# Splitting the second stage of a long convolution and its output stage into two halves of the channels

## The chip, the cores and the metric

The kernel runs on one core of one Trainium2 chip. The metric is the device time of one execution in microseconds (us). The kernel before takes 388.5 us (median of its first three runs, 388.43 to 392.61). Executions of the same kernel differ by 2 to 3 us either way, so smaller differences are read here from the traces and not from the times.

## The reference, cut to what matters

The output is two independent layers side by side, each 2048 steps by 1024 channels, in bf16.

```python
# A (H3): a long convolution over time, for each channel
kv  = shift(k, shift_k) * v                       # four taps
y_f = rfft(kv, 4096) * rfft(ssm_k, 4096)
a   = q * (irfft(y_f)[:2048] + kv * ssm_D)
# B (S5): a complex diagonal recurrence
Bu   = x @ B_bar.T
h[t] = Lam_bar * h[t-1] + Bu[t]
b    = 2 * (h @ C.T).real + x * Dskip
out  = concatenate([a, b], axis=-1)
```

## The kernel before

Layer A is a Fourier transform of length 4096 = 256 x 16, made of matmuls:

- Stage one transforms the signal (`am`) and the filter (`hm`) over the 256 and stores both in DRAM.
- Stage two takes 32 groups of frequencies. For each it loads both spectra, finishes the transform (`sh` filter, `sk` signal), swaps the real and imaginary partition halves of the filter spectrum by a transfer (`sw`), multiplies on VectorE (`pr`), transforms back (`sa`) and stores the inverse spectrum (`vst`).
- The output stage loads the inverse spectra (`vl`) and q (`ql`), does the last matmuls (`a3`), multiplies by q (`qm`, `qp`) and stores (`ost`, `oth`).

Layer B runs in 16 chunks of 128 steps: input projection `U`, rotation and scan on VectorE (`r1` to `r4`, `sc`), output projection `y`. It fills TensorE while layer A waits. ScalarE copies most results of TensorE out to SBUF (an "eviction"). A hand-written list of tasks fixes the order, and each engine runs its instructions in that order.

```python
ORDER = """ ... sk.31.0 sk.31.1 sae.28.1 y.12.0.0 cy.12 ske.31.0 ske.31.1 sa.29.0 sa.29.1 sae.29.0 sa.30.0 pr.31
sae.29.1 sa.30.1 sae.30.0 vst.14 sae.30.1 sa.31.0 sa.31.1 sae.31.0 y.12.0.1 sae.31.1 U.13.3 vst.15 U.15.0 ... """

def l_(nm, Ys, gq):                      # spectra of two groups, all 1024 channels: 512 KB
    if nm == "l2h":
        st[nm, gq] = btile("hk", [P, GC, D])
    else:
        st[nm, gq] = ap_pool("a2").tile([P, GC, D], BF16, name=nm, bufs=c["l2"])
    spd(st[nm, gq][:], Ys.rearrange("c n (s g) d -> (c n s) g d", g=NG)[:, gq * GC:(gq + 1) * GC, :])

def sw(g):                               # the swap, issued by GpSimd
    hab = st["hab", g]
    gpd(hab[0:64, 1, :], hab[64:128, 0, :])
    gpd(hab[64:128, 1, :], hab[0:64, 0, :])

def pr(g):                               # the product, on VectorE
    hab = st["hab", g]
    nc.vector.tensor_mul(hab[:], st.pop(("x16", g))[:].unsqueeze(1).to_broadcast([P, 2, D]), hab[:])

# ... cut ...
for task in ORDER.split():
    name, *a = task.split(".")
    E[name](*map(int, a))
```

`spd` issues a transfer from SyncE, `gpd` from GpSimd. The buffers of stage two (pool `a2`) and those of the output stage (pool `a3`) share the same memory, one after the other.

## Time and profile before

| | before |
|---|---|
| time, median | 388.5 us |
| span of the profiled execution | 386.9 us |
| TensorE / VectorE / ScalarE busy | 92% / 85% / 72% |
| work of TensorE, counted from the spacing of back-to-back matmuls | 352.2 us |
| span not filled by that work ("loss") | 34.7 us |

TensorE is the bound, so the question for any change is where TensorE stands still. The prediction shows the busy rows. Two further rows of the page: the clock granted to TensorE, in tenths for 40 slices, and the count of DMA packets.

```profile
PEclk9999999999999999999999999999999999999999
DMA packets 60506, 101.15 MB, mean 261 GB/s; under 512 B 28451, under 2 KB 31523, under 8 KB 60464
```

### The profile page before, as it was taken

Reading aid. Unit: us, or ns where it says so; the run is one execution under the profiler, and the core shown is the slowest. Engines: PE = TensorE matmul, PEld = TensorE weight load, DVE = VectorE, ACT = ScalarE, POOL = GpSimd, SP = SyncE. Lnnn points to the kernel's source line nnn. Section 1 sums busy time; section 2 is a strip of 40 time slices with the busy share of each in tenths; the row PEclk is TensorE's granted clock in tenths of the full one; section 3 lists DMA queues with packets and bytes.
Section 4 is the critical chain, followed back from the end, with each engine's and each line's share of the span. In section 5 each row is a group of like instructions: output and inputs, shape, how many; then the busy total and the mean of one; then the engine's idle time right before and its main releaser. Section 6 shows DMA issues by size and latency. Waiting matters only on the chain.

```text
span 386.9 us, 8963 instructions
## 1 busy us (share of the span) xinstructions
PE 357.3 (92%) x3509; PEld 244.7 (63%) x3553; DVE 329.4 (85%) x341; ACT 279.2 (72%) x511; POOL 128.1 (33%) x223
## 2 busy tenths in 40 slices
PE   2798998989999998999979999999997999999995
PEld 1587997859587765778536555465553676864442
DVE  2799999999999999999389999995943793989944
ACT  3799579786968698964867888868897876245331
POOL 7001004355555548661323324323442331011220
PEclk9999999999999999999999999999999999999999
DMA  7998299998775935456899999989997643998984
GB/s 243 372 347 295 86 221 298 269 327 271 285 215 196 284 154 207 186 178 222 260 300 290 307 271 319 272 296 268 322 271 259 226 154 133 324 401 267 393 302 163
DMA packets 60506, 101.15 MB, mean 261 GB/s; under 512 B 28451, under 2 KB 31523, under 8 KB 60464
## 3 DMA queue, kind: packets, MB, share of 16 engines
q1 hardware_dynamic: 46512, 58.21, 50.0%
q0 software_dynamic: 13872, 42.35, 30.3%
q8 instruction: 28, 0.46, 0.5%
q14 instruction: 14, 0.11, 0.1%
q10 hardware_dynamic: 80, 0.01, 0.0%
HBM read 53.10 MB, written 33.55 MB: 224 GB/s over the span
## 4 chain that ended last, share of the span: by engine, by line
PE 71%; ACT 9%; DMA 8%; DVE 6%; issue 4%; POOL 0%; DVEq 0%; ACTq 0%
PE ps_u L468 24%; PE ps_y L524 22%; PE ps_a L716 6%; PE ps_a L674 6%; DMA hab<-hab 3%; PE ps_a L746 3%; PE ps_a L593 2%; PE ps_a L639 2%; PE ps_y L529 2%; DMA CT<-in_B_B_im_dram 2%; PE ps_t L617 2%; ACT BT L434 2%; DMA Ys_h<-ysbh 1%; PE ps_t L422 1%; ACT ysbh L647 1%
## 5 line engine op out<-in xcount | busy, mean ns | idle before, releaser
L524 PE MATMUL ps_y<-CT,h 128*128 128x512 bf16 x478 | 130.1, 379 | 2.8 <-ACT yo L539 1.6
L468 PEld LDWEIGHTS <-BT 128*128 128x128 bf16 x2048 | 118.2, 98 | 8.7 <-ACT BT L434 1.3
L468 PE MATMUL ps_u<-xT,BT 128*128 128x128 bf16 x2048 | 122.7, 219 | 0.8 <-ACT BT L434 0.8
L524 PEld LDWEIGHTS <-h 128*128 128x128 bf16 x512 | 46.9, 98 | 46.7 <-issue 0.2
L500 DVE TENSOR_TENSOR_SCAN h<-rtab,h 128x1024 bf16<-128x1024 f32 x32 | 71.5, 2275 | 0.2
L470 ACT CAST u<-ps_u 128x512 bf16<-128x512 f32 x64 | 38.1, 595 | 41.3 <-PE ps_u L468 41.3
L707 DVE TENSOR_TENSOR hab<-x,hab 128x2048 bf16<-128x2048 bf16 x32 | 38.5, 1220 | 24.2 <-DMA hab<-hab 15.9
L654 POOL DMA_DIRECT2D Ys_h<-ysbh x64 | 45.4, 713 | 33.4 <-ACT ysbh L647 33.2
L480 DVE TENSOR_TENSOR mt<-u,Z 128x4096 bf16<-128x4096 bf16 x16 | 36.6, 2285 | 9.4 <-ACT u L470 9.4
L727 ACT CAST vsb<-ps_a 128x512 bf16<-128x512 f32 x64 | 36.8, 600 | 10.5 <-PE ps_a L716 7.6
L647 ACT CAST ysbh<-ps_a 128x512 bf16<-128x512 f32 x64 | 36.4, 619 | 8.2 <-DMA Ys_h<-ysbh 5.6
L604 POOL DMA_DIRECT2D Ys_kv<-ysb x32 | 17.8, 557 | 65.3 <-ACT ysb L602 64.9
L696 ACT CAST x<-ps_a 128x512 bf16<-128x512 f32 x64 | 36.8, 598 | 3.1 <-PE ps_a L674 2.9
L602 ACT CAST ysb<-ps_a 128x512 bf16<-128x512 f32 x64 | 36.4, 611 | 3.5 <-PE ps_a L593 3.5
L716 PE MATMUL ps_a<-hab,wts 128*128 128x512 bf16 x122 | 34.8, 379 | 4.2 <-DVE hab L707 4.1
L684 ACT CAST hab<-ps_a 128x512 bf16<-128x512 f32 x64 | 36.4, 600 | 2.1 <-PE ps_a L674 1.9
L701 POOL DMA_DIRECT2D hab<-hab x32 | 16.9, 527 | 60.1 <-ACT hab L684 59.7
L480 DVE TENSOR_TENSOR mt<-h,Z 128x4096 bf16<-128x4096 bf16 x16 | 36.6, 2286 | 0.2
L569 DVE TENSOR_TENSOR mt<-kring,wbc 128x4096 bf16<-128x4096 bf16 (+3 forms) x16 | 30.1, 1881 | 0.0
L539 ACT CAST yo<-ps_y 128x512 bf16<-128x512 f32 x32 | 19.1, 598 | 15.1 <-PE ps_y L524 15.1
L529 PE MATMUL ps_y<-Dd,xT 128*128 128x128 bf16 x128 | 28.0, 219 | 0.6
L639 PE MATMUL ps_a<-hT,F1t 128*128 128x256 bf16 x128 | 21.7, 272 | 1.6 <-ACT ysb L602 0.8
(118 smaller groups left out, 453.8 us busy)
## 6 DMA issues: line engine op xcount, KB each, us to landing
Ys_kv<-ysb POOLq DMA_DIRECT2D x32, 256.0 KB, 2.8
Ys_h<-ysbh POOLq DMA_DIRECT2D x64, 128.0 KB, 3.1
hk<-Ys_h SPq DMA_DIRECT2D x16, 512.0 KB, 6.3
l2k<-Ys_kv SPq DMA_DIRECT2D x16, 512.0 KB, 5.1
hab<-hab POOLq DMA_DIRECT2D x64, 128.0 KB, 4.2
Vs<-vsb POOLq DMA_DIRECT2D x16, 512.0 KB, 4.7
vv<-Vs SPq DMA_DIRECT2D x32, 256.0 KB, 5.5
hk<-in_A_ssm_k_dram SPq DMA_DIRECT2D x8, 512.0 KB, 4.8
```

The lines of the kernel that those rows point to most:

```text
L468: nc.tensor.matmul(pu[:, w, jl, :], BT[:, 2 * jp + jl, w, d, :], xT[:, d, :], start=(d == 0), stop=(d == ND - 1))
L470: E["ue"] = lambda i, jp: nc.scalar.copy(st["u", i][:, :, 2 * jp:2 * jp + 2, :], st.pop(("pu", i, jp))[:])
L480: nc.vector.tensor_mul(m, s_, win(Z))
L500: nc.vector.tensor_tensor_scan(gf[:, a * W:(a + 1) * W], rt1, gf[:, a * W:(a + 1) * W], 0.0, ALU.mult, ALU.add)
L524: nc.tensor.matmul(py[:], h[:, 1 - w, j, :], CT[:, j, w, dh * 512:(dh + 1) * 512], start=(j == 0 and w == 0), stop=(j == NJ - 1 and w == 1))
L602: nc.scalar.copy(st["ysb", n2, cc][:, dh * 512:(dh + 1) * 512], st.pop(("pa", n2, w))[:])
L647: nc.scalar.copy(st["yh", qd, n4, w // 2][:, :, w % 2, :], st.pop(("pa", qd, n4, w))[:].rearrange("p (c d) -> p c d", c=2))
L654: gpd(Ys_h[cc, n0:n0 + 2, :, qd * DQ:(qd + 1) * DQ].rearrange("n k d -> k n d"), t_[:, cc, :, :])
L696: nc.scalar.copy(st["x16", g][:, w * 512:(w + 1) * 512], st.pop(("ps", "l2k", g, w))[:])
L707: nc.vector.tensor_mul(hab[:], st.pop(("x16", g))[:].unsqueeze(1).to_broadcast([P, 2, D]), hab[:])
L716: nc.tensor.matmul(pt[:], st["w", gq][:, gi, 1 + a, :], hab[:, a, w * 512:(w + 1) * 512], start=(a == 0), stop=(a == 1))
L727: nc.scalar.copy(st["vsb", gq][:, gi, w * 512:(w + 1) * 512], st.pop(("ps", "v", g, w))[:])
```

## The change

Stage two and the output stage run in two halves of 512 channels. Groups 0 to 15 are the first half and 16 to 31 the second, in mirrored order, each with two frequency groups of one half. The output stage of the first half (`a3.0` to `a3.7`) can then run among the spectra of the second half. The intent is to fill TensorE at the change of stages and to leave only chunk 15 of the scan for the end. The price: the weights of stage two are loaded twice (29 loads for 16), pieces of transfers become 1 KB, buffers are re-cut, and the task order is tuned anew from the first task on.

```diff
-           hT=2, ysbh=2, l2=3, wts=4, swa=0, x16=4, hab=4, vsb=2, vv=7, qt=6, ot=5, bdve=8)
+           hT=2, ysbh=2, l2=2, wts=4, wsh=3, vw=5, qw=4, ow=3, swa=0, x16=3, hab=4, vsb=3, vv=2, qt=2, ot=2, bdve=8)
 ... (the whole ORDER is new: cut)
+    phases = (("a1",), ("a3a", "a2"), ("a3b",))      # a3b takes the place of a2; a3a stays
+    def gpair(g):
+        return 31 - g if g > 15 else g
+    def quad(Ys, gq):
+        a = 2 * min(gpair(2 * gq), gpair(2 * gq + 1))
+        return Ys.rearrange("c n (s g) d -> (c n s) g d", g=NG)[:, a:a + 4, (gq // 8) * 512:(gq // 8 + 1) * 512]
-        spd(st[nm, gq][:], Ys.rearrange("c n (s g) d -> (c n s) g d", g=NG)[:, gq * GC:(gq + 1) * GC, :])
+        spd(st[nm, gq][:], quad(Ys, gq))
+    def lw_(g):
+        st["w", g] = btile("wts", [P, GC, 3, P])
+        a = GC * gpair(g)
+        spd(st["w", g][:], W3v[:, a:a + GC, :, :])
+        if 16 - c["wsh"] <= g < 16:
+            st["w", 31 - g] = st["w", g]
+    def a3tile(tag, n, shape):
+        return atile("a3b" if n > 7 else "a3a", {"vv": "vw", "qt": "qw", "ot": "ow"}[tag] if n > 7 else tag, shape)
 ... (s2, pr, sa, vst, vl, ql, a3, qm, ost: the same operations on [P, 2, 512] tiles: cut)
```

## The prediction

> **What bounds the kernel now.** I first read the page's busy shares and its row of 40 slices, to see which engine is full and where it has holes.
>
> ```profile
> PE 357.3 (92%) x3509; PEld 244.7 (63%) x3553; DVE 329.4 (85%) x341; ACT 279.2 (72%) x511; POOL 128.1 (33%) x223
> ...
> PE   2798998989999998999979999999997999999995
> PEld 1587997859587765778536555465553676864442
> DVE  2799999999999999999389999995943793989944
> ```
>
> TensorE is full except at the start (two slices), at the change from the first to the second convolution stage (the 7 near 195 us), once late in the second stage (the 7 near 295 us) and in the last slice. VectorE (DVE) is full up to 180 us and has its holes after that. To turn "busy" into work I took the spacing of back-to-back matmuls from the chain that ended last: 32 of 128 columns take 1.79 us (56 ns each), 4 of 512 columns 0.86 us (216 ns each). With the counts (weight loads give the full counts, some matmul records are missing): 2048 input projections 114.3, 512 output projections 110.6, 256 second-stage matmuls 55.3, 64 first-stage and 64 output-stage matmuls 27.6, 128 filter matmuls 14.1, 128 skip matmuls 7.2, transposes and broadcasts about 23; together 352.4 us. The remaining 34.5 us of the span of 386.9 are what any reordering can win. The table by stretches splits them:
>
> ```profile
> 0.00:184.00 184.00, 166.87 (x2021) 132.92 (x2042) 174.03 (x209) 141.31 (x247) 73.31 (x120) 1.00 0.76 245
> 184.00:324.00 140.00, 134.06 (x1026) 77.84 (x1042) 108.52 (x89) 114.18 (x223) 45.62 (x86) 1.00 0.86 265
> 324.00:382.40 58.40, 56.42 (x466) 33.96 (x470) 45.98 (x43) 23.74 (x44) 9.21 (x17) 1.00 0.84 309
> 382.40:387.00 4.60, 0.00 (x0) 0.00 (x0) 0.87 (x2) 0.00 (x0) 0.00 (x0) 0.84 0.55 193
> ```
>
> The columns are the stretch, its length, busy time of PE, PEld, DVE, ACT and POOL, granted clock, DMA share, GB/s. Counting the work that the written order puts before its first second-stage matmul (162.4 us; that matmul starts at 183.9), before its last (295.8; about 323.6) and in all (352.4; 382.4), the losses are 21.5 us before stage two, 6.3 in it, 2.2 in the output stage, and 4.5 after the last matmul. So TensorE's work is the bound. The output stage, which the change breaks up, loses only 2.2 us: that is the point on which my prediction turns.
>
> **What the Trainium skill says.** "Perfetto Trace Analysis", section Identifying the Most-Contended Engine, says that matmul busy time misleads because matmuls are pipelined. The trace agrees mildly (357.3 busy for 352.4 of work), hence the count above. "DMA: Bandwidth & Descriptors", section Anatomy of one DMA, fits about 2.0 us plus bytes/436e3 for one transfer, 2.3 us for 128 KB. Here the swap of halves that each group needs, also 128 KB, takes longer under load, and I use these measured values:
>
> ```profile
> hab<-hab POOLq DMA_DIRECT2D x64, 128.0 KB, 4.2
> Vs<-vsb POOLq DMA_DIRECT2D x16, 512.0 KB, 4.7
> vv<-Vs SPq DMA_DIRECT2D x32, 256.0 KB, 5.5
> ...
> qt<-in_A_q_dram SPq DMA_DIRECT2D x16, 256.0 KB, 4.6
> ...
> wts<-a_c_W SPq DMA_DIRECT2D x16, 192.0 KB, 4.3
> ```
>
> (The last column is microseconds from issue to landing.) The same page, section Why small descriptors are slow, gives about 3 cycles of overhead for each packet beside one cycle per 32 bytes. That makes 1 KB pieces some 7% dearer than 4 KB ones, an estimate. The packet records agree in size: median 46 ns for 1,024 bytes, 84 for 2,048, 159 for 4,096.
>
> **The change part by part.** Counting the tasks of both orders: every compute instruction is there as often as before, with the same sizes. TensorE's 352.4 us, and the work of VectorE and ScalarE, do not change. Each task that covered 1,024 channels of one frequency group now covers 512 channels of two groups.
>
> Transfers: weight loads go from 16 to 29 (three are shared at the turn), +13 x 192 KB = 2.6 MB on 101. Spectrum loads come in pieces of 1 KB instead of 4 KB, loads of the inverse spectra and of q in 1 KB instead of 2. By the packet medians this costs 4 x 46 - 159 = 25 ns on each of some 4,096 packets, 8 ns on each of 6,144, and the new weights 13 x 128 packets of 65 ns: (102 + 49 + 108)/16 = 16 us of time on each of 16 queues, spread over 200 us. The stretch 200 to 280 us already has a DMA share of 0.96, yet TensorE was busy 78.6 of 80 us there, so I give contention little on its own. Stores of results become 32 of 256 KB; at about 0.55 us of issue each, POOL (33% busy) takes that.
>
> Moved: half of the output stage (6.9 us of TensorE, 8 of the 16 products) goes into stage two, which grows from 133.4 to about 163 us of TensorE work. Input and output projections of later chunks go with it: when the last spectrum product is made, the before order still has chunks 13 to 15 of the scan to do, the new one only chunk 15.
>
> Gains: between the first second-stage matmul and the first product (the wait in which TensorE lost 2.1 us in 190 to 200 us), the new order has 9.1 us of TensorE work instead of 7.7 and 9.7 us of VectorE work instead of 4.9; I take 1.5 off. Scaling the other 4.2 us of stage two by its work gives 5.1.
>
> Costs, each on TensorE's in-order path:
> 1. At the half boundary the first output matmul comes 10.4 us of work after the last spectrum matmul of that half. It needs the store (eviction and issue 1.2, landing 4.7) and the load (issue 0.5, landing 5.5) = 11.9. Loss 1.5. Before, this distance was about 14 us.
> 2. The end of the scan. After the last spectrum product VectorE does chunk 15 from the start. The trace has this chunk:
>
> ```profile
> 355.63 2.29 DVE L480 TENSOR_TENSOR mt<-u,Z 128x4096 bf16<-128x4096 bf16 x1
> ...
> 359.04 1.22 DVE L489 TENSOR_TENSOR h<-mt 128x2048 bf16<-128x2048 bf16 x1
> 360.30 0.23 DVE L494 TENSOR_TENSOR h<-h,carry 128x16 bf16<-128x16 bf16 x1
> ...
> 361.01 4.47 DVE L500 TENSOR_TENSOR_SCAN h<-rtab,h 128x1024 bf16<-128x1024 f32 x2
> 365.51 2.29 DVE L480 TENSOR_TENSOR mt<-h,Z 128x4096 bf16<-128x4096 bf16 x1
> 367.84 1.22 DVE L513 TENSOR_TENSOR h<-mt 128x2048 bf16<-128x2048 bf16 x1
> ```
>
> With the carry and one output product between them that is 2.3 + 0.2 + 0.7 + 1.2 + 0.2 + 4.5 + 2.3 + 1.2 = 12.6 us. The product itself cannot start before the last swap has landed: from the last filter matmul of the stage, eviction 1.5, two swap issues of 0.53, landing 4.2, product 1.2 = 8.0. So 20.6 us lie between that matmul and the first output projection of chunk 15. TensorE has 16.4 us of work in between. Loss 4.2.
> 3. The last loads. The second half's buffers take the place of stage two's, so its loads of q and of the spectra cannot be issued early, and five spectrum buffers serve eight loads. The eighth waits for the third tile's matmuls, which in the order stand only 2.2 us of work before its own; the seventh only 1.7. Issue and landing in a draining queue take some 5. Loss about 2.7. Before, these distances were mostly 10 to 15 us and no matmul of that line waited over 0.1 us in all.
>
> Sum: 352.4 + 21.5 + (0.6 + 5.1 + 1.5) + 4.2 + 2.7 + 4.5 = 392.5 us of span. The measured time stood 1.6 us above the span (388.5 and 386.9), giving 394.
>
> **The rivals.**
> (a) The order pays: chunk 15 alone at the end and better filled transitions remove the losses of stage two and the end bubble is filled. For it: 6.3 us lost there now. Against it: even all of that without new waits gives 386.9 - 6.3 = 380.6 of span, 382 measured, which is 1.6% and not 2%. Only a shorter start-up (10.9 us lost in the first 30) could add to it, and the new order starts alike: its first input projection stands after 7.2 us of TensorE work instead of 6.5.
> (b) Transfers become the bound of stage two. Each weight load now serves one group instead of two with the same four buffers: from its place in the order to its first use lie 7.4 us of TensorE work in the median (least 5.0) where there were 13.7, and for the signal spectra, with two buffers instead of three, 9.4 instead of 14.9. Landing is 4.3 and 5.1 in the median and 5.7 and 7.8 at most. With the whole stretch now at 300 GB/s and more, a microsecond or two on each swap would show on TensorE. If a third of the 32 groups each lose 0.7 us, that is 7 more: 401.
> (c) The transfer costs are hidden anyway and the DVE chain at the end is met by a TensorE that is already late; then losses 2 and 3 shrink to 2 together and the time is 389.
>
> **Range and chances.** The work of TensorE is unchanged and its 34.5 us of loss are mostly in start-up and first stage, which the change does not aim at. Faster by over 2% (below 380.7) needs more than everything in stage two and at the end: 0.04. (b) in part or in full takes it above 396.3: 0.33. The rest, 0.63, is within 2%, rather above than below. Range 387.5 to 401.5.
>
> **What would show it.** TensorE's work count equal to before; a wait of TensorE before the output projections of the last chunk of 3 to 6 us, released by VectorE; waits of the output-stage matmuls for the inverse spectra at the half boundary and in the last 8 us; fewer idle VectorE microseconds near 190 us. It is wrong in its main step if the last stretch has no such waits, and wrong in the other direction if second-stage matmuls wait for weights or swaps by more than 5 us in sum.

## More of the kernel before

The granted clock is 90% or more in every slice (0.998 in the mean). The end of stage one is dense too. Here are two stretches of it (columns: stretch, length, busy time of TensorE's matmuls, weight loads, VectorE, ScalarE and GpSimd, granted clock, DMA share, GB/s):

```profile
158.00:170.00 12.00, 11.89 (x138) 9.32 (x139) 12.00 (x13) 9.10 (x17) 6.77 (x11) 1.00 0.39 152
170.00:182.00 12.00, 11.95 (x162) 9.84 (x162) 11.79 (x11) 7.24 (x14) 5.20 (x9) 1.00 0.71 236
```

TensorE misses 0.16 us of 24, and the transfers leave room: DMA share 0.39 in the first stretch.

## The result, and the profile after

The changed kernel takes 405.1 us (median of 4 runs, 404.53 to 406.24), beside 389.1 us before. The ratio is 1.040, with a 95% interval of 1.034 to 1.046: slower. Ratios and intervals are for fast runs of both kernels in the same rounds; they are not quite the ratios of the quoted medians. The prediction, 394 us with a range up to 401.5, was wrong.

The same rows of the page, after:

```profile
PE 367.6 (91%) x3513; PEld 249.3 (62%) x3553; DVE 330.6 (82%) x341; ACT 280.4 (69%) x511; POOL 144.7 (36%) x239
...
PE   3799998999999998699999999979999998999683
...
PEclk9789999999999999879999999998999999999897
...
DMA packets 81069, 103.72 MB, mean 257 GB/s; under 512 B 28916, under 2 KB 62324, under 8 KB 81025
```

VectorE's and ScalarE's busy times are those of before. TensorE has the same 3553 weight loads but is "busy" 10 us longer, and the clock row shows why: there are dips below full speed near 20, 170 and 275 us and at the end, where before had none. The bytes grew by 2.6 MB and the small packets doubled, both as predicted. The stretches that answer to the prediction's table, cut at the first matmul of stage two, its last one, and TensorE's last:

```profile
0.00:195.60 195.60, 177.81 (x2054) 139.04 (x2071) 180.14 (x215) 143.32 (x249) 73.82 (x121) 0.97 0.78 236
195.60:366.30 170.70, 165.39 (x1358) 99.84 (x1378) 132.40 (x108) 128.28 (x248) 65.06 (x110) 0.99 0.90 278
366.30:399.40 33.10, 24.40 (x105) 10.45 (x106) 16.85 (x19) 8.76 (x16) 5.84 (x9) 0.90 0.85 282
399.40:403.80 4.40, 0.00 (x0) 0.00 (x0) 1.17 (x2) 0.00 (x0) 0.00 (x0) 0.73 0.44 153
```

Stage two is well filled, but the 33 us after it are not.

To place the loss I used the records of TensorE's weight loads, of which none is missing: each belongs to a task of the list. The time at which a task starts, less the work of all tasks before it, is the loss so far. The differences between marks are the losses by phase:

| TensorE's loss in us, from the mark before until | before | after |
|---|---|---|
| input projection of chunk 8 (about 160 us) | 21.8 | 20.8 |
| last stage-one matmul | 0.0 | 7.2 |
| first inverse matmul (`sa.0.0`) | 2.6 | 0.7 |
| inverse of group 15 | 1.2 | 3.7 |
| inverse of group 31 | 2.1 | 2.3 |
| first output projection of chunk 15 | 1.3 | 4.7 |
| last output projection of chunk 15 | 0.8 | 1.5 |
| last matmul | 0.2 | 6.2 |
| end of the span | 4.7 | 4.5 |
| sum | 34.7 | 51.6 |

The difference, 16.9 us, is that of the spans (403.8 and 386.9). Three places carry it: the last part of stage one (+7.2), chunk 15 (+4.1) and the last output matmuls (+6.0, with 0.2 back after them). TensorE's waits name the releasers (total, times, longest):

```profile
PE ps_a L738 <- DVE hab L730: 3.6, 3, 2.1
...
PE ps_a L603 <- ACT ysbh L657: 3.5, 3, 2.5
PE ps_y L534 <- DVE h L523: 3.5, 1, 3.5
...
PE ps_a L774 <- ACT ow L782: 2.3, 1, 2.3
PE ps_a L774 <- DVE ow L788: 1.9, 2, 1.5
```

**The end of stage one.** In the kernel before, SyncE issues the first filter spectra for stage two at 176.64. In the changed one a half needs only the first two quarters of the filter, so the loads depend on less and go out far earlier, from SyncE's own queue:

```profile
158.12 1.49 SPq L683 DMA_DIRECT2D hk<-Ys_h  x3
```

Those 1.5 MB then share the queues with the last filter stores. The chain that ended last has one such store in it, and the two stretches shown above for before now read:

```profile
161.82 7.67 DMA Ys_h<-ysbh
```

```profile
158.00:170.00 12.00, 7.55 (x85) 5.48 (x84) 12.00 (x13) 6.61 (x12) 5.90 (x9) 0.97 0.91 284
170.00:182.00 12.00, 11.72 (x97) 8.80 (x98) 11.78 (x10) 7.49 (x16) 5.90 (x9) 0.74 0.27 109
```

Such a store lands in 3.0 us in the median; the four issued from 158.2 to 161.8 took 4.8 to 7.9 us. ScalarE waited for the two `ysbh` buffers and TensorE for ScalarE. In the second stretch TensorE looks full again, but it did 98 weight loads in place of 162: the granted clock was 0.74. In the trace's clock records a halved stretch lasts 3.41 or 6.83 us (one or two "windows" from here on), except where the run's end cuts it; here it lasts from 169.3 to 176.2.

**The halved clock** follows the long waits of the changed kernel: it is halved at 15.7 to 22.6, 169.3 to 176.2, 271.7 to 275.1, 377.6 to 381.0, 394.6 to 398.0 and from 401.4 on. The Trainium skill, "TensorE: Matmul & The Clock Gate", section HAM oscillation — how this bites in real kernels, gives the rule "no PE-idle gaps >~3.4µs". Here a wait of 2.06 us was enough once, but not always: in e8 below the same wait, 2.06 us at 271.3, was followed by no halved window, nor were the kernel before's waits of 2.05 and 2.07 us. In all sixteen traces together, after the first 30 us, all 11 waits above 3.3 us go with a halved window that begins during the wait or within 1.2 us of its end; of the 30 waits of 2.0 to 3.0 us, 17 do. Span times (1 - clock) is 7 to 13 us in the four runs of the changed kernel and 0 to 3 us in those of the kernel before; it is an upper bound on the cost, because part of it falls into idle time.

**Near 271 us**, the transposing load of input chunk 15 (issued at 261.10, landed at 269.53) meets the swaps of groups 13 to 15. The swap of group 13 took 7.9 us to land; its 64 packets of 4 KB took 469 ns in the median where 159 ns is usual. VectorE and then TensorE waited:

```profile
270.12 1.23 DVE L730 TENSOR_TENSOR hab<-x,hab 128x2048 bf16<-128x2048 bf16 x1 [3.19 <-DMA hab<-hab]
...
271.40 0.74 PE L738 MATMUL ps_a<-hab,wts 128*128 128x512 bf16 x2 [2.06 <-DVE hab L730]
```

**Chunk 15.** The wait that the prediction named is there; in brackets, the idle time and its releaser:

```profile
377.29 0.39 PE L534 MATMUL ps_y<-CT,h 128*128 128x512 bf16 x1 [3.46 <-DVE h L523]
```

**The last output matmuls.** The second half has three output buffers (`ow=3`), and they wait for their stores:

```profile
393.98 1.07 ACT L782 CAST ow<-ps_a 128x512 bf16<-128x512 f32 x2 [2.92 <-DMA out_dram<-ow]
394.62 2.72 PE L774 MATMUL ps_a<-vw,Gt 128*128 128x512 bf16 x6 [2.34 <-ACT ow L782]
...
398.83 0.38 PE L774 MATMUL ps_a<-vw,Gt 128*128 128x512 bf16 x1 [1.50 <-DVE ow L788]
```

### The profile page after: what moved, and what is told of

Same layout as the page of the kernel before. It is cut to its first block, busy times and chain, and to the rows that moved or that the text cites. A ratio compares the mean times of both kernels' runs of the same rounds, so it can differ in the third digit from the quotient of the medians.

```text
span 403.8 us, 9059 instructions
## 1 busy us (share of the span) xinstructions
PE 367.6 (91%) x3513; PEld 249.3 (62%) x3553; DVE 330.6 (82%) x341; ACT 280.4 (69%) x511; POOL 144.7 (36%) x239
## 4 chain that ended last, share of the span: by engine, by line
PE 67%; DMA 16%; DVE 6%; ACT 5%; issue 2%; POOL 1%; SPq 1%; DVEq 0%; ACTq 0%; POOLq 0%
PE ps_u L478 22%; PE ps_y L534 21%; PE ps_a L697 5%; DMA hab<-hab 5%; PE ps_a L738 5%; DMA CT<-in_B_B_re_dram 4%; DMA Ys_h<-ysbh 4%; PE ps_a L649 3%; PE ps_a L603 3%; PE ps_a L774 2%; PE ps_t L432 2%; DVE mt L490 2%; PE ps_y L539 2%; DMA vv<-Vs 1%; PE ps_t L627 1%
## 5 line engine op out<-in xcount | busy, mean ns | idle before, releaser
L534 PE MATMUL ps_y<-CT,h 128*128 128x512 bf16 x489 | 133.1, 385 | 5.4 <-DVE h L523 3.5
L478 PEld LDWEIGHTS <-BT 128*128 128x128 bf16 x2048 | 121.3, 99 | 9.8 <-issue 1.2
L478 PE MATMUL ps_u<-xT,BT 128*128 128x128 bf16 x2048 | 126.6, 221 | 0.1
L749 POOL DMA_DIRECT2D Vs<-vsb x32 | 23.1, 721 | 57.9 <-ACT vsb L747 56.7
L747 ACT CAST vsb<-ps_a 128x512 bf16<-128x512 f32 x64 | 35.3, 598 | 10.5 <-PE ps_a L738 7.8
L738 PE MATMUL ps_a<-hab,wts 128*128 128x512 bf16 x120 | 32.4, 380 | 3.6 <-DVE hab L730 3.6
```

The lines of the kernel that those rows point to most:

```text
L478: nc.tensor.matmul(pu[:, w, jl, :], BT[:, 2 * jp + jl, w, d, :], xT[:, d, :], start=(d == 0), stop=(d == ND - 1))
L534: nc.tensor.matmul(py[:], h[:, 1 - w, j, :], CT[:, j, w, dh * 512:(dh + 1) * 512], start=(j == 0 and w == 0), stop=(j == NJ - 1 and w == 1))
L738: nc.tensor.matmul(pt[:], st["w", g][:, w, 1 + a, :], hab[:, a, w * 512:(w + 1) * 512], start=(a == 0), stop=(a == 1))
```

## The experiments

My theory after the result: the work and the bytes cost nothing in themselves; the loss is made by a few waits, each caused by where a transfer stands or how few buffers follow it, and lengthened by the halved clock. Rivals: the added transfers slow everything; or the structure itself (half of layer A's output only after the last spectrum) costs the time wherever the tasks stand. Fourteen kernels ran, and each passed the comparison with the reference. None of them separates the split itself from the new task order and buffers that came with it. TensorE's losses by phase in all of them (fillers counted as work; "stage one" is up to chunk 8's projection, "filter" from there to the last stage-one matmul, "entry" to the first inverse, the two halves to inverses 15 and 31, "ch. 15" both its rows, then the output matmuls and what follows the last one):

| kernel | stage one | filter | entry | half 1 | half 2 | ch. 15 | output | after | time, us | ratio to before |
|---|---|---|---|---|---|---|---|---|---|---|
| before | 21.8 | 0.0 | 2.6 | 1.2 | 2.1 | 2.1 | 0.2 | 4.7 | 389.1 | 1 |
| after | 20.8 | 7.2 | 0.7 | 3.7 | 2.3 | 6.2 | 6.2 | 4.5 | 405.1 | 1.040 |
| e1 | 20.4 | 0.8 | 2.4 | 5.8 | 2.3 | 6.2 | 6.9 | 5.1 | 406.9 | 1.048 |
| e2 | 19.6 | 5.7 | 1.1 | 4.8 | 2.2 | 1.8 | 6.5 | 4.7 | 402.9 | 1.038 |
| e3 | 21.4 | 6.9 | 0.5 | 3.3 | 3.1 | 6.2 | 1.3 | 7.2 | 401.5 | 1.034 |
| e4 | 20.6 | 5.9 | 1.0 | 2.0 | 3.0 | 5.7 | 6.2 | 5.1 | 405.0 | 1.044 |
| e5 | 21.3 | 0.8 | 2.7 | 6.2 | 3.4 | 2.2 | 3.5 | 6.7 | 405.0 | 1.042 |
| e6 | 22.1 | 0.0 | 2.1 | 1.5 | 0.9 | 2.1 | 0.2 | 4.4 | 387.9 | 0.998 |
| e7 | 19.8 | 5.8 | 1.5 | 0.3 | 4.8 | 5.8 | 6.3 | 4.7 | 401.4 | 1.032 |
| e8 | 22.1 | 6.0 | 0.5 | 2.0 | 4.7 | 3.3 | 6.4 | 4.9 | 404.1 | 1.043 |
| e9 | 19.8 | 5.9 | 0.7 | 2.3 | 3.5 | 7.7 | 1.1 | 6.9 | 403.7 | 1.042 |
| e10 | 21.1 | 0.8 | 3.5 | 1.1 | 5.7 | 2.9 | 1.5 | 7.5 | 398.2 | 1.025 |
| e11 | 19.4 | 6.0 | 1.0 | 3.2 | 5.1 | 5.7 | 1.1 | 6.9 | 403.4 | 1.042 |
| e12 | 21.7 | 0.0 | 3.3 | 32.5 | -0.2 | 2.1 | 0.2 | 4.7 | 419.2 | 1.075 |
| e13 | 20.9 | 0.8 | 2.7 | 0.3 | 5.1 | 3.5 | 1.6 | 5.0 | 394.2 | 1.011 |
| e14 | 22.6 | 0.8 | 4.1 | -0.1 | 4.6 | 6.0 | 1.1 | 5.5 | 398.7 | 1.020 |

The kernel before stood at 388.0 to 390.3 (medians) beside these runs. The phases come from one profiled execution each. In e9, e11, e12 and e14 one run of four was slow; their times are medians of the other three. e11's three fast runs alone give 1.036.

### e1: the first spectrum loads behind the filter stores

```diff
-        spd(st[nm, gq][:], quad(Ys, gq))
+        (gpd if nm == "l2h" and gq < 3 else spd)(st[nm, gq][:], quad(Ys, gq))
```

GpSimd issues the filter stores in order, so the loads now stand behind them.

> Edit: the first three loads of filter spectra go out on the queue of the stores, behind the last filter stores, instead of 1.5 MB ahead of them. Theory: in the changed kernel these early loads (possible because half the channels depend on the first two filter quarters alone) held up filter stores (one took 7.7 us against a median of 3.0), ScalarE waited for the buffer, TensorE fell idle and its clock was halved from 169 to 176 us; then the loss of TensorE time between 158 and 180 us falls from 8.6 to 2 us or less, no halved clock near 170 us, and the time falls by 5 to 7 us, to 398 to 400. Rival: the DMA transpose of an x tile just before (256-byte packets) is what slowed the stores; then the loss stays at 6 us or more and the time at 403 to 406.

Measured: 406.89 us (403.95 to 409.27). The filter phase lost 0.8 us, no window was halved near 170, and the stretches are nearly dense again (1.5 us missing of 24):

```profile
158.00:170.00 12.00, 10.64 (x136) 8.54 (x135) 12.00 (x13) 9.85 (x19) 7.75 (x12) 1.00 0.51 191
170.00:182.00 12.00, 11.89 (x129) 8.61 (x129) 11.93 (x11) 8.44 (x17) 7.30 (x12) 1.00 0.38 154
```

So the cause of this phase's loss is shown: the early loads were in the way of the stores. But the time did not fall. TensorE came to stage two some 6 us earlier, and there entry and first half lost 8.2 us in place of 4.4. TensorE waited 2.21 us for a product at 202.2, and 3.92 us for one at 268.6, where the swap of group 13 took 9.8 us beside the transposing load of chunk 15 (10.6 us in flight). What was left of the gain lies within the spread of the runs.

### e2: TensorE kept busy before chunk 15

```diff
         py = st["py", i, dh]
+        if (i, dh, part) == (15, 0, 0):
+            for _ in range(12):  # results are overwritten
+                nc.tensor.matmul(py[:], F1t[:, 0, :], CT[:, 0, 0, 0:512], start=True, stop=True)
```

> Edit: twelve throw-away matmuls of 512 columns (2.6 us) on TensorE while it waits for VectorE before the output projections of the last chunk. Theory: the wait itself costs 3.5 us, and costs more because the idle time halves the granted clock for the next 3.4 us; with the filler the projections start when they did (about 377.3 us) but at full clock: no halved stretch from 377.6 on, time 1.5 to 2 us less, 403 to 404. Rival: the halved clock there lies in the shadow of the loads and buffers that bound the end; then the clock is restored but the time stays within 0.5 us of 405.

Measured: 402.93 us (401.49 to 404.71). The fillers took the place of the wait:

```profile
373.20 2.75 PE L534 MATMUL ps_y<-CT,F1t 128*128 128x512 bf16 x12 [0.67 <-ACT yo L552]
```

No window was halved near 377. Chunk 15 lost 1.8 us plus 2.6 of filler, 4.4 against 6.2. The saving of 1.8 us is about the worth of one halved window of 3.4 us; in time it is at the edge of the spread.

### e3: deep buffers at the end

```diff
-vw=5, qw=4, ow=3
+vw=7, qw=6, ow=6
-                if o != "a3a":
+                if o != "a3a" or name == "a3b":
```

> Edit: the pool of the first half's outputs is closed when the second half's opens; the freed SBUF goes to 7 spectrum, 6 q and 6 output buffers instead of 5, 4 and 3. Theory: with 3 output buffers the last output tiles wait for stores to land (ScalarE 2.9 us, VectorE 2.3 us, TensorE 2.3 and 1.5 us after 390 us) and TensorE falls idle into a halved clock; then these waits go, and the time falls by 3 to 5 us, to 400 to 402. The prediction's own version: the waits are for the spectrum loads; then the same fall, but the waits that vanish are those on the spectra. Rival: the end is set by the scan of the last chunk and the output projections alone; then under 1 us.

Measured: 401.54 us (399.23 to 403.72). TensorE's loss in the output matmuls fell from 6.2 to 1.3, which shows that the buffers caused it; the last waits there are now short:

```profile
392.79 1.07 PE L774 MATMUL ps_a<-vw,Gt 128*128 128x512 bf16 x3 [0.18 <-ACT ow L782]
...
394.13 0.59 PE L774 MATMUL ps_a<-vw,Gt 128*128 128x512 bf16 x2 [0.28 <-DMA vw<-Vs]
```

The loss after the last matmul rose from 4.5 to 7.2. The DMA share was 1.03 to 1.06 from 377 to 395 (packets are counted where they start, so a share can exceed 1), so I took the rest for a bound by transfers; e9, e11 and e13 test this.

### e4: chunk 12 out earlier

The four parts of `y.12.1` were moved ahead (behind `sh.25.1`, `sh.26.1`, `sk.25.1` and `sh.27.1`), with `ye.12.1` and `yst.12`, and `qm.5 ql.7 ost.5` behind `sc.14`.

> Edit: the second half of chunk 12's output projections is moved ahead by about 15 us of TensorE work, and one output product of VectorE (with its load and store) behind the scan of chunk 14. Theory: the chain that leads to TensorE's wait before the last chunk starts where chunk 14's state buffer comes free (two buffers; chunk 12's last projection), at 350 us, from where VectorE runs without a gap to 377; starting it earlier by 3 to 6 us removes the wait of 3.5 us and the halved clock after it: time 3 to 5 us less, 400 to 402. Rival (the prediction's version): the chain starts at the last swap of halves and its product; then chunk 14 starts earlier but the wait before the last chunk stays at 3 us or more, and the time within 1 us of 405.

Measured: 404.98 us (403.0 to 408.51). The second step of chunk 14's rotation (`r2`) began at 344.4 instead of 350.15, but the wait before chunk 15 was still 3.0 us (3.46 in the changed kernel). VectorE now stood idle for the last swaps instead. So the chain that the prediction named, last swap, last product, chunk 15, sets this wait, more than the shortage of `h` buffers.

### e5: e1, e2 and e3 together

> The changed kernel with the three earlier edits together: the first three spectrum loads behind the filter stores, 12 throw-away matmuls before the last chunk, deep output buffers at the end. If the losses are separate, their effects add: the end of the filter stage loses about 1 us instead of 7, the wait before chunk 15 about 0.8 plus 2.6 of filler instead of 4.7, the last output matmuls 1.3 instead of 6.2, with 2.5 given back after the last matmul and 3 to 4 in the first half of stage two: a span of 395 to 398, a time of 396 to 399. Rival: every microsecond won early is given back at the end, because the second half's loads can start only after the last spectrum store and then fill the queues: then the time stays at 400 to 402, as in the run with deep buffers alone, and the loss after the last projection of chunk 15 grows above 10 us.

Measured: 404.98 us (403.46 to 406.27), a miss. Filter and chunk 15 did what they did alone; the output matmuls lost 3.5 us in place of e3's 1.3. Entry and first half lost 8.9 us: near 260 the swaps took 7.5 to 9.3 us while the transposing load of chunk 15 ran from 258.4 to 268.6. And 10.2 us were lost after chunk 15, as the rival said.

### e6: the transfers of the change in the kernel before

```diff
-        spd(st[nm, gq][:], Ys.rearrange(...)[:, gq * GC:(gq + 1) * GC, :])
+        for h in range(2):
+            spd(st[nm, gq][:, h, :, :], Ys.rearrange(...)[:, gq * GC:(gq + 1) * GC, h * 512:(h + 1) * 512])
         spd(st["w", gq][:], W3v[:, gq * GC:(gq + 1) * GC, :, :])
+        if gq > 3:  # a second load of the same weights, into a tile that nothing reads
+            spd(ap_pool("a2").tile([P, GC, 3, P], BF16, name="wdup", bufs=2)[:], W3v[:, gq * GC:(gq + 1) * GC, :, :])
 ... (the tiles' shapes and the matmul's index follow; arguments of rearrange: cut)
```

> The kernel before, in its own order, with the transfer costs of the change: spectra loaded in pieces of 1 KB by two loads instead of one, and 12 of the 16 weight loads done twice, the second time into a tile that nothing reads. My theory: the added transfers cost little by themselves, at most 1.5 us (below 390.5), with stage two losing at most 1.5 us more than before; the loss of the change is in its order and its buffers. Rival: the added bytes and small packets are the cause; then this kernel loses 4 us or more in stage two and stands at 393 or above.

Measured: 387.89 us (385.21 to 390.63), ratio 0.998 (0.992 to 1.005). Stage two lost 4.5 us, against 5.9 in the kernel before. The rival falls: the second load of the weights and the spectra in 1 KB pieces cost nothing that can be measured in an order that leaves room for them. (The loads of q and of the inverse spectra in 1 KB pieces were not tested.)

### e7: the transposing load of chunk 15 later

`x.15` was moved behind `pr.19`.

> The changed kernel with the transposing load of the last input chunk moved behind product 19, away from the swaps of groups 12 and 13. Theory: that load is what made those swaps slow and TensorE lose 2.1 us at 271 and then a window at the halved clock: the loss between first product and inverse 15 falls from 3.7 to 1.5 to 2, no halved clock near 272, and 2 us less in time (403). Rival: the queues are full there in any case; then swaps of groups 12 to 15 still wait over 2 us and the loss of that stretch stays above 3.

Measured: 401.43 us (400.59 to 402.78). The first half lost 0.3 us in place of 3.7, and no window was halved near 272. The product of group 13, which had waited 3.19 us for its swap, now starts without a wait:

```profile
265.95 1.22 DVE L730 TENSOR_TENSOR hab<-x,hab 128x2048 bf16<-128x2048 bf16 x1
```

The swaps of groups 13 to 15 still took 4.8 to 7.5 us with no transposing load in flight, so that load is not their only brake. With e3 this is the largest single gain in time, 3.7 us against the changed kernel's 405.1 (in other rounds). Some of it came back at once: the second half lost 4.8 in place of 2.3.

### e8: the first rotation of chunk 15 earlier

As e4, with `r1.15` moved before `pr.30`.

> The changed kernel with chunk 12 out earlier (as in the run before) and the first rotation of chunk 15 moved ahead of product 30, into the time in which VectorE waited 1.4 us for swaps. Theory: VectorE's path from the last products to chunk 15 shortens by about 2 us, the wait before chunk 15's projection falls from about 3 to 1 to 1.5 us, below what triggers the halved clock, so the three phases from inverse 31 to the end of chunk 15 lose 4 us or less instead of 8.5; time 401 to 403. Rival: the last products are delayed by the rotation and the last chain of the spectra is met later: the wait stays at 3 or more.

Measured: 404.13 us (403.37 to 409.25). The chunk-15 phases lost 3.3 us in place of 6.2, with no halved window there, as expected. But the second half lost 2.4 us more, so the sum of 8.0 missed my 4 or less. Its cause is open: TensorE's longest wait there was 1.44 us for a load of the inverse spectra at 297.0 (0.3 us in the changed kernel), before the moved tasks; its waits for products were 0.5 us.

### e9: q early, and deep buffers without closing the first half's pool

```diff
-vw=5, qw=4, ow=3
+vw=6, ow=6
-        st["qt", n] = a3tile("qt", n, [P, 2, 512])
+        if n in (8, 9, 10, 11, 13):  # in buffers that earlier chunks and spectra have left
+            st["qt", n] = btile("xT", [P, ND, T])[:].rearrange("p (a b) t -> p a (b t)", a=2)
+        elif n > 7:
+            st["qt", n] = btile("hk", [P, 4, 512])[:, 0:2, :]
+        else:
+            st["qt", n] = a3tile("qt", n, [P, 2, 512])
```

> The changed kernel with the loads of q for the second half issued before the last spectra, into buffers that earlier input chunks and spectra have left, and with the room of the q buffers given to six buffers each for the inverse spectra and the results; the first half's pool stays open, so the spectra are loaded as soon as their stores are out. In the run with deep buffers TensorE lost 1.3 us up to its last matmul but 7.2 after it, the queues at a share of 1. Theory: the end was bound by what had to be loaded and stored after the last spectrum, 2.1 MB of q among 8.9; without them the two phases after chunk 15 lose 5 to 6.5 us instead of 10.7 (changed kernel) or 8.5 (deep buffers), time 399 to 401. Rival: the chain from the last inverse spectrum to its store sets the end and q does not matter: 8 us or more remain, time 401 to 403. The phases before inverse 31 should stay as they are (35 us); if they rise by 2 or more, the early loads of q disturb the swaps.

Measured: 403.7 us (402.02 to 406.94; a fourth run, slow, took 408.63; the profiled one, 402.02, was the fastest). The output phase kept its gain (1.1), but 6.9 us stayed after the last matmul: 8.0 in sum, where I expected 5 to 6.5. Chunk 15 lost 7.7 us in place of 6.2. The theory of the transfers did not hold here.

### e10: all repairs together

e1, e7, e8 and e9 in one kernel.

> All repairs in one kernel, still in two halves: spectrum loads behind the filter stores, chunk 15's transposing load late, chunk 12 and the rotation of chunk 15 early, q early and deep buffers. If the losses named so far are all there is: filter stage 0.8, entry and first half of stage two 2.5 to 4, second half 2 to 4, chunk 15 wait 3 or less, the end 5 to 6.5: about 37 to 40 us of loss, a span of 389 to 392, a time of 391 to 394, level with the kernel before and not faster. Rival: repairs push each other's gain to the next wait, as in the run of three together: time 397 or more.

Measured: 398.16 us (395.37 to 398.44), ratio 1.025 (1.018 to 1.031). It is better than any single repair and 4 us above what I hoped; 5.7 us were lost in the second half and 7.5 after the last matmul.

### e11: half the inverse spectra at the end (wrong)

On top of e9, the second half loads only the real spectra and uses them twice:

```diff
-        for cc in range(2):
+        for cc in range(2 if n < 8 else 1):
...
-Gt[:, cc, :], st["vv", n][:, cc, w, :]
+Gt[:, cc, :], st["vv", n][:, cc if n < 8 else 0, w, :]
```

> Wrong on purpose: the kernel with early q and deep buffers, but the output stage of the second half loads only the real spectra and uses them twice, so 2.1 MB less has to come in after the last spectrum store. TensorE does the same matmuls. Theory: the end is bound by those transfers (share of the queues about 1 until the last matmul), so the loss after the last matmul falls from 6.9 to about 4.7, as in the kernel before, the wait of chunk 15 stays at 4 to 5, and the two phases after chunk 15 lose 5 to 6 instead of 8. Rival: the end is bound by the stores of the last outputs alone: 6.5 or more stay after the last matmul.

Measured: 403.4 us (402.44 to 404.55; a fourth run, slow, took 409.35), 1.1 and 6.9 us in the two last phases, exactly as in e9. My theory of the end fell. (The comparison passed this kernel, which computes something else; so it is not sharp enough to vouch for layer A. The other kernels change no arithmetic.) What then set the end? The last transfer landed at 396.72, 3.8 us before the span's end at 400.55. The last line of this kernel's program shows the closing instructions (minimum, median and longest in ns, then first and last start):

```profile
L858 POOLq DRAIN  x3: 51/107/6930, 392.8 to 400.3; - x3
```

GpSimd's closing DRAIN began at 392.8 with GpSimd's last DMA issue and took 6.93 us. All engines waited for it. In the kernel before, the same line reads:

```profile
L825 POOLq DRAIN  x3: 51/107/3900, 380.5 to 386.6; - x3
```

There it was over at 384.4, before the last landing (385.36). The Trainium skill, "Perfetto Trace Analysis", section DMA Instruction — SWDGE (GPSIMD), says that the recorded end of such a transfer is the end of descriptor generation, not of the data's move. The trace agrees: GpSimd's last store is recorded from 392.84 to 393.56 and landed at 395.64. It goes further: over all sixteen kernels, the DRAIN ended 1.5 to 1.9 us after the landing of GpSimd's last transfer in the order of the kernel before, and 3.1 to 4.6 us after it in the halved kernels.

### e12: five gaps in the kernel before

```diff
+    def gapl():
+        nc.gpsimd.dma_start(cst("gapt", [64], BF16)[:], x[0:P, 0:64])
+    def gapm():  # reads the tile, so the next load waits for TensorE, and TensorE then for that load
+        nc.tensor.matmul(ptile("ps_t", [P, 512])[:, 0:64], ident[:], cst("gapt", [64], BF16)[:], start=True, stop=True)
+    # one gapl behind yst.5, and "gapm gapl gapm" behind y.6.1.3, y.7.0.3, y.7.1.3, y.8.0.3 and y.8.1.3
```

> The kernel before, with five gaps put into TensorE's work in the first half of stage two, about 10 us apart: each a small load that waits for a throw-away matmul and is waited for by another, so TensorE stands still for some 2.5 to 3.5 us each time. It measures what a wait of that size costs by itself. Theory: part of the gaps is followed by a window of 3.4 us at the halved clock, costing about 1.7 us more each, so the loss up to inverse 15 exceeds the summed waits by 3 to 8 us, and the time grows by 16 to 24 us. Rival: the halved clock needs a longer or different idle time; then no window near the gaps is halved and the loss is the sum of the waits, 12 to 17 us, or less where other waits are absorbed.

Measured: 419.2 us (416.06 to 420.57; a fourth run, slow, took 422.43), 30 us above the kernel before in the same rounds where I expected 16 to 24. The waits were longer than I meant them to be:

```profile
221.20 0.21 PE L548 MATMUL ps_t<-gapt,ident 128*128 128x64 bf16 x1 [5.59 <-DMA gapt<-in_B_x_dram]
...
232.65 0.20 PE L548 MATMUL ps_t<-gapt,ident 128*128 128x64 bf16 x1 [2.24 <-DMA gapt<-in_B_x_dram]
...
248.79 0.20 PE L548 MATMUL ps_t<-gapt,ident 128*128 128x64 bf16 x1 [2.92 <-DMA gapt<-in_B_x_dram]
...
262.28 0.23 PE L548 MATMUL ps_t<-gapt,ident 128*128 128x64 bf16 x1 [5.91 <-DMA gapt<-in_B_x_dram]
...
281.38 0.23 PE L548 MATMUL ps_t<-gapt,ident 128*128 128x64 bf16 x1 [7.54 <-DMA gapt<-in_B_x_dram]
```

They add up to 24.2 us, while the first half lost 31.3 us more than in the kernel before. The excess of 7.1 us (the ten throw-away matmuls are counted as 2.2 us of work) I put down to the halved clock: windows at 219.5 to 226.3, 233.1 to 236.6, 260.5 to 267.3 and 277.5 to 284.3. Of these, 16.5 us lie after the waits, and half of that is 8.2. The theory holds: the halved clock follows from waiting as such, not from the change. The wait of 2.24 us was followed by a halved window and the one of 2.92 us was not. Counting windows of 3.41 us on from 233.1, the former fell wholly into one window and the latter was split 0.9 to 2.0 between two. This grid is an estimate of mine from the halved stretches.

### e13: all repairs, and GpSimd's last two stores issued by SyncE

```diff
-E["ost"] = lambda n: gpd(part(oar, n), st.pop(("ot", n))[:])
+E["ost"] = lambda n: (spd if n in (11, 12) else gpd)(part(oar, n), st.pop(("ot", n))[:])
```

> The kernel with all repairs, except that the stores of outputs 11 and 12 are issued by SyncE instead of GpSimd, so GpSimd's last transfer is issued some 4 us earlier. Theory: GpSimd's closing DRAIN of 7 to 8 us ends the kernel; it then ends at about 391 instead of 395.4, the last landing (392 to 393) sets the end, the time after the last matmul falls from 7.5 to 4.7 to 5.3, and the time from 398.2 to about 395.5 to 396.5. Rival: the DRAIN only waits for whatever lands last; then it stretches to the last landing and beyond and 7 us or more stay after the last matmul.

Measured: 394.23 us (394.07 to 395.57), ratio 1.011 (1.004 to 1.017). The DRAIN started earlier, at 381.7, and was over at 390.7, before the last landing at 391.3:

```profile
L858 POOLq DRAIN  x3: 51/99/9059, 381.7 to 392.0; - x3
```

The time after the last matmul fell from 7.5 to 5.0 us, as expected; the DRAIN grew to 9.06 us but no longer ended last. So GpSimd's late stores set the end in e10. (That is 2.5 of the 3.9 us between the two profiled spans; the rest lies in phases that the edit does not touch, and the two kernels ran in different rounds.) This is the best halved kernel: within 2% of the kernel before, still 1.1% slower.

### e14: e13, with the spectrum loads late on SyncE and chunks 12 and 15 unmoved

`lh.0 lh.1 lh.2` on SyncE behind `x.11`, without e8's moves.

> As the run before, but the first three spectrum loads are issued late by SyncE instead of by GpSimd behind the filter stores, and chunk 12 and the rotation of chunk 15 stay in the places that the change gave them. Theory: with the loads out of GpSimd's queue the first swaps land in 3 to 6 us instead of 7.5 to 8.4 and the entry of stage two loses 1 to 2 us instead of 3.5, while the filter stage still loses about 1; the second half loses 2 to 3.5 as in the changed kernel and the wait before chunk 15 is 4 to 5 again: time 394 to 397. Rival: the swaps are slow because all 16 engines are full with the spectra, whoever issues them: 3 us or more at the entry.

Measured: 398.7 us (396.85 to 399.46; a fourth run, slow, took 404.6), ratio 1.020 (1.010 to 1.031), unclear at 2%. The first four swaps (the later of their two transfers) did land in 3.1 to 6.9 us in place of 6.9 to 8.8, but then the first spectrum came late (TensorE waited 2.8 us for it), and the entry lost 4.1. Both my sides were half right: the loads must come before the swaps, and they slow the stores if they come earlier still. Chunk 15 lost 6.0 again, where e13 with e8's moves lost 3.5.

## Why the prediction was wrong, point by point

The sum of the prediction was a span of 392.5 us; it became 403.8. The terms, with what they measured:

| term of the sum | predicted | measured |
|---|---|---|
| work of TensorE | 352.4 | 352.2 |
| loss before stage two | 21.5 | 28.0 |
| loss in stage two | 7.2 | 6.7 |
| chunk 15 | 4.2 | 6.2 |
| last loads and output matmuls | 2.7 | 6.2 |
| after the last matmul | 4.5 | 4.5 |

**The step that failed** is "21.5 us before stage two", which the prediction carried over from the kernel before, with only the remark that "the new order starts alike" for the start-up. The end of stage one was never looked at. Half a spectrum depends on half of the filter, so its loads became ready some 18 us earlier and ran into the filter stores; the trace shows it and e1 proves it (7.2 to 0.8 us in that phase). e1 also shows that the loss is not simply additive: alone, its removal did not shorten the run measurably (406.9 us). With TensorE on time, entry and first half of stage two lost 3.8 us more: 1.7 at the entry, where the likely reason is that the lost 6 us had given the first swaps time to land, and 2.1 in the first half, where the transposing load now held TensorE for 3.92 us. Once that load was out of the way too (e13), entry and first half lost only 3.0. The other large miss, "last loads", is below.

**Contention.** "I give contention little on its own" was right for the added bytes (e6: ratio 0.998) and wrong as a reading of the whole. The median transfer hardly slowed (swap 4.4 us for 4.2 before). What cost were single collisions: three loads against the filter stores, one transposing load against three swaps (e7: 3.4 us of loss). An argument from medians cannot see these.

**Stage two, 7.2.** Right in size, 6.7; but the composition was partly luck, since the entry gained 1.9 us and the first half lost 2.5 more. Of the 1.5 us foreseen at the half boundary, TensorE's waits for the inverse spectra there show 0.6. Rival (b), every group losing a little to late transfers, did not happen: weights were not waited for.

**Chunk 15, 4.2.** The mechanism was right, to the releaser: one wait of 3.46 us for VectorE, and e4 shows that the last swap and product come before it. The size was short by 2.0 us; e2 shows that 1.8 us of that is the halved clock, which I had not thought of at all.

**Last loads, 2.7.** Mis-sized, and put down only in part to the right buffers. I counted the five spectrum buffers, and one weight load did wait 1.59 us for a spectrum that landed at 393.33. But TensorE's matmuls waited 2.3 and 1.9 us for the three output buffers behind slow stores, which I had not counted; e3, which deepened all three kinds, shows only that the buffers together make the difference of 4.9 us.

**The end, 4.5.** The number, carried over from the kernel before, held, but what stands behind it changed. Before, SyncE's last store ended the kernel; in the changed kernel, GpSimd's DRAIN (396.05 to 402.98) and the last landing (402.47) come almost together. In e3, e5, e9, e10 and e11 the DRAIN ended 2.0 to 3.1 us after the last landing and hid part of what the repairs had gained.

**Of the rivals**, (a) and (c) fell with the result. What remains open: why e13 still lost 5.1 us in the second half (2.1 before); TensorE's waits there, for evictions, loads of the inverse spectra and a product, sum to 2.3 us, none above 0.9. And why the DRAIN takes longer in the halved kernels is not shown; their stores have 1 KB pieces, but no run tested that alone. Nor did I run the changed kernel with the DRAIN's repair alone. No halved version beat the kernel before.

My reading of what is left, which no run tests: the structure itself has a limit that the repairs did not remove. After the last inverse matmul, TensorE has 57 us of work left in the kernel before (352.2 - 295.2), and 21 us in the changed one (352.2 - 331.1), with half of the output stage still to load, multiply and store. So the change seems to have traded a long, well covered end for fuller middle stages that lost only 6 us to begin with.

## What to carry to other kernels

When a change splits work into parts, look at what becomes ready earlier, not only at what waits longer: an early load can push aside a store that somebody needs, and the place to look is the stage before the one that changes. Sum the waits of the critical engine by phase, and look in the clock records for a halved window after each wait of 2 us or more (28 of 41 such waits had one here). Look at what really ends last: here a GpSimd DRAIN behind its last store hid 2.5 us of repairs until two stores moved to another issuing engine.

## What the Trainium skill lacked or had wrong

- "TensorE: Matmul & The Clock Gate", section HAM oscillation — how this bites in real kernels: the bound of 3.4 us for idle gaps is too lax here. Waits of 2.06 and 2.24 us were each followed by a halved window of 3.4 us; one of 2.92 us was not. Over all sixteen traces, 17 of the 30 waits of 2.0 to 3.0 us went with one. The halved clock often lasted two windows (6.8 us, three times in e12 and twice in the changed kernel). It cost about 1.8 us for one window in e2.
- "Perfetto Trace Analysis", section DMA Instruction — SWDGE (GPSIMD): nothing says that GpSimd's closing DRAIN can end the kernel. It ran 3.9 us from the last issue in the kernel before, 6.8 to 9.1 us in the halved kernels, and ended up to 3.1 us past the last landing; moving two stores to SyncE took 2.5 us off.
- "DMA: Bandwidth & Descriptors", section Anatomy of one DMA: its fit for one transfer gives 2.3 us for each 128 KB of a swap and has no term for other transfers in flight. The trace has 2.2 us at the least, but 4.2 us (before) and 4.4 us (after) in the median and up to 9.8 us beside a transposing load.
- No page that I read says how a transposing load slows other transfers in flight: the 4 KB packets of one swap took 469 ns in the median beside it, against 159 ns. It is not the only brake: in e7 the swaps of groups 13 to 15 took 4.8 to 7.5 us with no transposing load in flight.
